# An attention and gated-MLP kernel: the last chunk's gate values kept in SBUF instead of DRAM, its last copies moved to ScalarE, its final adds split over GpSimd and VectorE

## The chip, the cores and the metric

The kernel runs on one core of a Trainium2 chip, in one launch. The metric is the device time of one execution in microseconds; the time before is the median of seven runs. The engines are named as in the profile: PE (TensorE), with its weight loads apart as PEld, DVE (VectorE), ACT (ScalarE), POOL (GpSimd) and SP (SyncE, which here only issues DMAs).

## The reference

All inputs and the output are bf16. With S = 2048 tokens, D = 640, 32 heads of 20 columns and F = 1728:

```python
xn = layernorm(x)
q, k, v = split(xn @ wqkv)                    # 32 heads of 20
o = softmax(q @ k.T * 20 ** -0.5) @ v         # every token with every token
s = o @ wo
h = sigmoid(xn @ w_gate) * (xn @ w_up)
g = silu(h @ w_down)
out = x + s * g
```

## The kernel before

**The tiling.** The tokens lie in four chunks of 512 (`QC`, index c), each of four token tiles of 128 (t4). The heads lie in eight groups of four (g). A *block* is one group with one chunk of queries: 32 blocks in all, in the order of the groups, but with the last two groups interleaved, so that the chunks end one after another; block 31 is the last group with the last chunk (c = 3). A block computes the scores of four heads against 16 key tiles on PE (L881, one matmul of 32 rows for each head, into the PSUM banks `scA` and `bk`), their exponentials, and the product with the values (L918, a *value group* of PE), which adds up in the PSUM bank `oacc`. v carries a column of ones, so row 0 of each head in `oacc` is the softmax's denominator.

**Two ways to the exponential.** Some of the score tiles go to ACT, which takes exp from PSUM (L120, output `pt`). The others go to DVE, which approximates exp on the bits of the numbers: one conversion to int16 for each 512 columns (L1214, output `iv`), and then three passes over up to four of them at a time (L966, L969, L972, output `pb`).

**What is put between.** The gated MLP runs as filler work on PE: for each chunk the gate and up products (L698, into `hT` over ACT's tanh and a product on DVE), then the down product (L736) for each token tile and each half of the 640 columns. `mk_down` ends with ACT's tanh of the result (L120, output `td`) and DVE's product (L746), which leaves the gate values times four, in fp32, in a small rotating tile `gqs`. A DMA on SP (L748) writes that tile to a DRAM scratch, `gq_dram`. For the chunks 0 to 2, `mk_out` later multiplies o with wo (L786), reads the gate values back (L772) and combines them with x (L793 on DVE, L796 on POOL), and L798 stores the result.

**The division.** After a block, DVE copies `oacc` to SBUF (L931). The denominators go through DRAM and a reciprocal (L941), come back broadcast (`rl`, L946), POOL multiplies (L948), and SP writes the result to `oU` (L956), which is the left operand of the product with wo. For block 31 this is done on the core instead, as the *chain*: DVE copies `oacc` (`e_on`, L1006), PE transposes (L1010), DVE takes the reciprocal (L760) and multiplies (L762), PE transposes back (L1019), and DVE copies the result to `o` (`e_o`, L1023).

**The end.** The output product of the last chunk lies in PSUM: 512 columns of each of the four token tiles in `mains` (two in `scA`, two in `bk`), and the remaining 128 columns of all four in one bank, `rest`. The `fill` list multiplies all heads but the last group's (L997), and `late_mm` adds the last group's (L1001), the rest first and then the mains. `tail_load` reads, for each of the four token tiles, x (L985) and the gate values (L986) from DRAM into the region of `wd`, which is free once the last down product is over. Then DVE multiplies the rest by the gates (L1043) and adds x (L1048), and for each token tile multiplies (L1052) and adds (L1055, tiles 0 to 2 on POOL, tile 3 on DVE). L1059 stores the four tiles, from SP and ACT in turn.

**What sets the order.** PE, ACT and DVE run in an order that a planner writes out when the program is built: it steps through time with a cost for each piece of work and takes, for each engine, what is ready. `PLAN` holds one row of its settings for each block; they take effect when the block becomes the first with scores still to claim. POOL and SP are not among the planner's engines: their instructions are placed by the scheduler, by what they depend on, and each of the two runs its own queue in order. Tiles from a pool rotate over a fixed number of buffers by their tag: `gqs` and `otmp` share one tag of three buffers, and the weight tiles of the projections share the tag `wp` of two, whose last users are the loads `load_wu` of the last two units and the matmuls on them (L558, and `qu`, whose results L607 writes to `qD`).

Of the kernel before, what the change touches and what calls it, by code (L numbers as in the profile page):

```python
# [10 lines left out]
FP32 = mybir.dt.float32  # L11
BF16 = mybir.dt.bfloat16
I16 = mybir.dt.int16
ACT = mybir.ActivationFunctionType
ALU = mybir.AluOpType
# [3 lines left out]
P = 128  # L19
HEADS = 32  # L20
GH = 4
NG = HEADS // GH
DH = 20
GC = GH * DH
QC = 512
# [47 lines left out]
)  # L73

LOG2E = 1.4426950408889634
# [14 lines left out]
def kernel(  # L90
# [11 lines left out]
    nc = tc.nc  # L102
    x2 = A_x[0] if len(A_x.shape) == 3 else A_x
    out2 = out[0] if len(out.shape) == 3 else out
    S, D = x2.shape
    assert D == HEADS * DH and S % QC == 0
    KD = D // P
# [4 lines left out]
    NQC = S // QC  # L112
    HD = D // 2
# [16 lines left out]
    wk = ctx.enter_context(tc.tile_pool(name="wk", bufs=2))  # L130

    gq_dram = dram.tile([S, D], FP32, name="gq_dram", tag="gqd", bufs=1)
# [8 lines left out]
    vts = [persist.tile([P, TT, 2 * GH, VW], BF16, name=f"v{i}") for i in range(2)]  # L141
# [97 lines left out]
    with tc.tile_pool(name="ln", bufs=2) as lp, \  # L239
# [159 lines left out]
        t = 0.0  # L399
# [19 lines left out]
    w2 = ctx.enter_context(tc.tile_pool(name="w2", bufs=2))  # L419
# [7 lines left out]
    oacc = psum.tile([P, QC], FP32, name="oacc", tag="oacc")  # L427
# [24 lines left out]

    out_tiles = {}
    xfl = xnT.rearrange("p c k q -> p (c k q)")

# [12 lines left out]
    NBLK = NG * NQC  # L468
# [11 lines left out]
    q_at = {0: 0.0}  # L480
# [247 lines left out]
    def mk_down(c, t4, h, at):  # L728
        st = {}
        tt = 4 * c + t4  # L730

        def alloc():
            st["ps"] = misc_ps()

        def mm(kf):
            nc.tensor.matmul(st["ps"][:, 0:HD], lhsT=hT[0:fsz[kf], kf, t4 * P:(t4 + 1) * P],  # L736
                             rhs=wd[0:fsz[kf], kf, h * HD:(h + 1) * HD],
                             start=(kf == 0), stop=(kf == NFT - 1))

        def th():  # L740
            st["td"] = w2.tile([P, HD], BF16, tag="td", bufs=2, name="td")
            act_imm(st["td"], st["ps"][:, 0:HD], ACT.Tanh, 0.25)

        def ev():
            gqs = w2.tile([P, HD], FP32, tag="gqs", bufs=3, name="gqs")
            nc.vector.scalar_tensor_tensor(out=gqs, in0=st["td"], scalar=1.0, in1=st["ps"][:, 0:HD],  # L746
                                           op0=ALU.add, op1=ALU.mult)
            nc.sync.dma_start(out=gq_dram[tt * P:(tt + 1) * P, h * HD:(h + 1) * HD], in_=gqs)  # L748
        return Item([("PE", alloc, [(0.14, lambda kf=kf: mm(kf)) for kf in range(NFT)]),
                     ("ACT", 0.32, th), ("DVE", 0.40, ev, "free", mark("d", c, t4, h))], at, pre=[("h", c, kf) for kf in range(NFT)])  # L750

# [62 lines left out]
    items = [mk_v(0, list(range(t, min(t + 3, TT))), 0.0) for t in range(4 * NVP, TT, 3)]  # L814
    for b in range(NBLK):
        g, c = gc(b)
# [21 lines left out]
    glu_items = [x for f in glu for x in f(0.0)]  # L838
# [7 lines left out]
    def base():  # L846
        while head_blk[0] < NBLK - 1 and not n_left[head_blk[0]]:
            head_blk[0] += 1
        return head_blk[0]
# [125 lines left out]
    wfl = wd.rearrange("p k s -> p (k s)")  # L975
    hfl = hT.rearrange("p k s -> p (k s)")
    EX = D - 512
    tail = []

    def tail_load():  # L980
        for t4 in range(4):
            r = slice(4 * (NQC - 1) * P + t4 * P, 4 * (NQC - 1) * P + (t4 + 1) * P)
            o2 = wfl[:, t4 * 3 * D:(t4 + 1) * 3 * D]
            tail.append((o2[:, 0:D], o2[:, D:3 * D].bitcast(FP32)))
            nc.sync.dma_start(out=tail[t4][0], in_=x2[r, :])  # L985
            nc.sync.dma_start(out=tail[t4][1], in_=gq_dram[r, :])  # L986

# [3 lines left out]
    mains = [scA[1][:, 0, :], scA[1][:, 1, :], bank[0], bank[1]]  # L991
    rest = bank[2]
    last = {}
# [9 lines left out]

    def e_on():
        last["on"] = w2.tile([P, QC], FP32, tag="on", bufs=2, name="on")
        nc.vector.tensor_copy(out=last["on"], in_=oacc)  # L1006

    def e_tr():
        for i in range(4):
# [10 lines left out]

    def e_o():
        last["o"] = w2.tile([GC, QC], BF16, tag="rl", bufs=1, name="o7")
        nc.vector.tensor_copy(out=last["o"], in_=last["t"][0:GC, 0:QC])  # L1023

    chain = [("DVE", 0.60, e_on), ("PE", 1.52, e_tr), ("DVE", 0.75, e_scale), ("PE", 0.42, e_back), ("DVE", 0.45, e_o)]
    fill = []
    for kds in (range(t_l - 1), range(t_l - 1, t_l + 1)):
        fill += [(t4 - 2, 0.2133, lambda t4=t4, kd=kd: early(mains[t4], t4, slice(0, 512), kd))
# [4 lines left out]
    def tail_steps():  # L1033
        for _, _, f in fill:
            f()
        for t4 in range(4):
            late_mm(rest[:, t4 * EX:(t4 + 1) * EX], t4, slice(512, D))
        for t4 in range(4):
            late_mm(mains[t4], t4, slice(0, 512))
        tmps = [hfl[:, t4 * 2 * D:t4 * 2 * D + 1024].bitcast(FP32) for t4 in range(4)]  # L1040
        xg = wfl[:, 0:12 * D].rearrange("p (t u) -> p t u", u=3 * D)
        tmp = hfl[:, 8 * D:8 * D + 8 * EX].bitcast(FP32)
        nc.vector.scalar_tensor_tensor(out=tmp.rearrange("p (t e) -> p t e", e=EX),  # L1043
                                       in0=rest.rearrange("p (t e) -> p t e", e=EX), scalar=0.25,
                                       in1=wfl[:, 0:12 * D].bitcast(FP32).rearrange(
                                           "p (t u) -> p t u", u=3 * D // 2)[:, :, D // 2 + 512:3 * D // 2],
                                       op0=ALU.mult, op1=ALU.mult)
        nc.vector.tensor_tensor(out=xg[:, :, 512:D], in0=tmp.rearrange("p (t e) -> p t e", e=EX),  # L1048
                                in1=xg[:, :, 512:D], op=ALU.add)
        for t4 in range(4):  # L1050
            xr, gqr = tail[t4]
            nc.vector.scalar_tensor_tensor(out=tmps[t4], in0=mains[t4], scalar=0.25, in1=gqr[:, 0:512],  # L1052
                                           op0=ALU.mult, op1=ALU.mult)
            add = nc.vector if t4 == 3 else nc.gpsimd
            add.tensor_tensor(out=xr[:, 0:512], in0=tmps[t4], in1=xr[:, 0:512], op=ALU.add)  # L1055
        for t4 in range(4):
            r = slice(4 * (NQC - 1) * P + t4 * P, 4 * (NQC - 1) * P + (t4 + 1) * P)
            eng = nc.sync if t4 % 2 == 0 else nc.scalar
            eng.dma_start(out=out2[r, :], in_=tail[t4][0])  # L1059

    with tc.manual_schedule(engines={ENG.PE, ENG.Activation, ENG.DVE}):
        nc.sync.dma_start(out=wo, in_=A_wo.rearrange("(kd p) e -> p kd e", p=P))
# [7 lines left out]
        now = 0.0  # L1070
# [13 lines left out]
        active = []  # L1084
# [38 lines left out]
        while chain or items or glu_items or any(it.i < len(it.ops) for it in active):  # L1123
# [3 lines left out]
            if bb > blk_loaded:  # L1127
                blk_loaded = bb
                rule.update(zip(KEYS, PLAN[bb]) if bb < len(PLAN) else ())
                g, c = gc(bb)  # L1130
                if c == 0 and g + 1 < PG:
                    spread_wst(g + 1, load_wst(g + 1))
                if c == 0 and g + 1 < NG:
                    if g % 2 == 1:
                        wvs[(g + 1) // 2] = load_wv((g + 1) // 2)
            if not tail and not glu_items and q_at.get(NBLK - 1, 1e9) <= now and not any(
                    it.need is None for it in items + active):
                tail_load()
            active = [it for it in active if it.i < len(it.ops)]
            if u_next < NU and base() >= (PG + u_next * UH // GH - 1) * NQC - 3 and (  # L1140
# [18 lines left out]
            for eng in ("ACT", "DVE"):  # L1159
# [15 lines left out]
                if it is not None:  # L1175
                    op = run_item(it, eng)
# [242 lines left out]
```

## Time and profile before

| what | value |
|---|---|
| median of 7 runs | 827.22 us (825.82 to 829.71) |
| profiled execution | 829.71 us, span 828.0 us |
| mean granted TensorE clock | 0.988 |
| instructions | 17089 |
| L120, `pt` from `scA` on ACT, x712 | 704.5 us busy |
| L1214, `iv` on DVE, x496 | 328.4 us busy |
| L881, score matmuls on PE, x1420 and x628 | 277.3 and 204.3 us busy |
| L1055, `wd` on POOL, x3 | 3.8 us busy |
| `gq_dram<-gqs` on SP | 32 issues, 160.0 KB each |
| DMA | 62.66 MB, mean 76 GB/s |

The profile is of one execution, and all positions in it are microseconds from the start of its span. "Busy" of PE counts matmuls that overlap in the pipeline. The chain of waits follows the work that ended last back from its end: each line has a start, a length, the engine, the tile written and the line. In the timeline, a bracket behind an instruction gives the idle time of its engine ahead of it and what released it. In the table of stretches, each column is an engine's busy time with the number of instructions in brackets, then the granted PE clock, the busy share of the DMA engines, and GB/s.

### The profile page before, as it was taken

The numbers are of one execution on the slowest core, as the hardware profiler recorded it, in microseconds if no ns is written. First come the engines' busy times: TensorE is split into PE (matmuls) and PEld (weight loads), VectorE is DVE, ScalarE is ACT, GpSimd is POOL, SyncE is SP. The second block draws the span as 40 slices with busy tenths as digits, with TensorE's granted clock in tenths as the row PEclk, the third lists the DMA queues.
The fourth block names the chain that finished last, engine by engine and source line by source line (L and its number), as shares of the span: only waits on it lengthen the run. The fifth ranks groups of instructions, "written<-read, shape, count | busy, mean of one in ns | idle before, by whom it ended". The sixth has DMA issues, their size and how long they took to land.

```text
span 828.0 us, 17089 instructions
## 1 busy us (share of the span) xinstructions
PE 787.2 (95%) x6420; PEld 269.6 (33%) x6420; DVE 780.6 (94%) x1230; ACT 785.5 (95%) x989; POOL 86.7 (10%) x90
## 2 busy tenths in 40 slices
PE   4799999999999999999999999999999999999994
PEld 2432222333333333333323222333333223333331
DVE  7689999999999999999999999999999999999992
ACT  7699999999999999999999999999999999999970
POOL 5000000000000000000000010000000002131141
PEclk9899999999999999999999999999999999999997
DMA  5611221123221232222112213331321124322214
GB/s 156 192 35 47 65 80 43 52 64 78 61 69 52 69 83 73 75 54 74 44 50 69 69 50 83 90 93 46 86 63 55 52 81 128 104 79 93 65 57 146
DMA packets 94899, 62.66 MB, mean 76 GB/s; under 512 B 36356, under 2 KB 88196, under 8 KB 94816
## 3 DMA queue, kind: packets, MB, share of 16 engines
q1 hardware_dynamic: 94528, 61.24, 26.4%
q8 instruction: 50, 0.82, 0.4%
q10 hardware_dynamic: 288, 0.33, 0.1%
q14 instruction: 33, 0.27, 0.1%
HBM read 46.59 MB, written 12.40 MB: 71 GB/s over the span
## 4 chain that ended last, share of the span: by engine, by line
PE 40%; ACT 30%; DVE 21%; issue 6%; DMA 2%; SPq 1%; POOL 0%; POOLq 0%; DVEq 0%; ACTq 0%
ACT pt L120 27%; PE scA L881 12%; PE oacc L918 8%; DVE iv L1214 8%; PE bk L698 8%; DVE pb L972 4%; PE bk L736 4%; DVE pb L966 2%; DVE pb L969 2%; PE bk L666 2%; PE bk L558 1%; ACT tnh L120 1%; PE bk L786 1%; DVE hT L706 1%; PE bk L881 1%
## 5 line engine op out<-in xcount | busy, mean ns | idle before, releaser
L120 ACT ACTIVATE pt<-scA 128x1024 bf16<-128x1024 f32 x712 | 704.5, 1149 | 7.7 <-PE bk L881 4.5
L1214 DVE TENSOR_SCALAR iv<-bk 128x512 int16<-128x512 f32 x496 | 328.4, 678 | 12.2 <-PE bk L881 11.3
L881 PE MATMUL scA<-q,kT 32*128 32x512 bf16 x1420 | 277.3, 384 | 7.8 <-ACT pt L120 3.7
L881 PE MATMUL bk<-q,kT 32*128 32x512 bf16 x628 | 204.3, 384 | 1.0 <-DVE iv L1214 0.7
L918 PE MATMUL oacc<-pt,v 128*21 128x512 bf16 x1552 | 182.0, 383 | 0.0
L881 PEld LDWEIGHTS <-kT 32*128 32x128 bf16 x2048 | 85.5, 91 | 261.8 <-issue 251.2
L918 PE MATMUL oacc<-pb,v 128*21 128x512 bf16 x992 | 156.5, 382 | 0.4 <-DVE pb L972 0.3
L972 DVE TENSOR_TENSOR pb<-iv,pb 128x2048 bf16<-128x2048 bf16 x124 | 154.4, 1246 | 0.7
L698 PE MATMUL bk<-xnT,wgu 128*128 128x512 bf16 x520 | 150.2, 383 | 2.1 <-DVE iv L1214 1.1
L948 POOL TENSOR_TENSOR on_bf<-on,rl 128x512 bf16<-128x512 f32 x31 | 46.2, 1489 | 665.3 <-DMA rl<-rd 396.9
L120 ACT ACTIVATE pt<-bk 128x512 bf16<-128x512 f32 x132 | 95.0, 720 | 1.4 <-PE bk L881 1.1
L966 DVE TENSOR_SCALAR pb<-iv 128x2048 int16<-128x2048 int16 x124 | 89.9, 725 | 1.2
L969 DVE TENSOR_SCALAR pb<-iv 128x2048 int16<-128x2048 int16 x124 | 90.9, 733 | 0.0
L736 PE MATMUL bk<-wd,hT 128*128 128x320 bf16 x448 | 88.1, 303 | 1.1 <-DVE iv L1214 0.9
L918 PEld LDWEIGHTS <-v 128*21 128x21 bf16 x2544 | 50.0, 91 | 88.9 <-issue 64.8
L698 PEld LDWEIGHTS <-wgu 128*128 128x128 bf16 x520 | 36.7, 97 | 66.5 <-issue 51.0
L736 PEld LDWEIGHTS <-hT 128*128 128x128 bf16 x448 | 34.1, 97 | 47.1 <-issue 38.9
L558 PE MATMUL bk<-xnT,wu 128*128 128x512 bf16 x160 | 47.0, 383 | 0.3 <-DVE iv L1214 0.3
L120 ACT ACTIVATE tnh<-bk 128x512 bf16<-128x512 f32 (+1 forms) x56 | 41.0, 731 | 0.1
L706 DVE SCALAR_TENSOR_TENSOR hT<-tnh,bk 128x512 bf16<-128x512 bf16 x52 | 35.2, 678 | 1.5 <-PE bk L698 0.8
L666 PE MATMUL bk<-wv,xnT 128*128 128x160 bf16 x280 | 29.5, 247 | 0.7 <-DVE iv L1214 0.6
L796 POOL TENSOR_TENSOR xnT<-otmp,xnT 128x320 bf16<-128x320 f32 x24 | 23.5, 987 | 46.9 <-DVE otmp L793 46.8
(105 smaller groups left out, 364.7 us busy)
## 6 DMA issues: line engine op xcount, KB each, us to landing
rl<-rd SPq DMA_DIRECT2D x124, 64.0 KB
wgu<-in_B_w_gate_dram SPq DMA_DIRECT2D x24, 320.0 KB
wgu<-in_B_w_up_dram SPq DMA_DIRECT2D x24, 320.0 KB
gq_dram<-gqs SPq DMA_DIRECT2D x32, 160.0 KB
xnT<-gq_dram SPq DMA_DIRECT2D x12, 320.0 KB
xt<-in_A_x_dram SPq DMA_DIRECT2D x16, 160.0 KB
oU<-on_bf SPq DMA_DIRECT2D x108, 20.0 KB
wd<-in_B_w_down_dram SPq DMA_DIRECT2D x1, 2080.0 KB
```

The source lines that it names most:

```text
L120: return nc.scalar.add_instruction(mybir.InstActivation(func=func, name=nc.get_next_instruction_name(), engine=ENG.Activation, ins=[nc.sca ...
L558: nc.tensor.matmul(st["ps"], lhsT=wus[u][:, kd, i, :], rhs=xnT[:, c, kd, :], start=(kd == 0), stop=(kd == KD - 1))
L666: nc.tensor.matmul(st["ps"][:, i * 2 * GC:(i + 1) * 2 * GC], lhsT=xn_tok(tts[i], kd), rhs=wvs[pr][:, kd, :], start=(kd == 0), stop=(kd == ...
L698: nc.tensor.matmul(st[key][0:fs, :], lhsT=w[:, i, kd, ko * P:ko * P + fs], rhs=xnT[:, c, kd, :], start=(kd == 0), stop=(kd == KD - 1))
L736: nc.tensor.matmul(st["ps"][:, 0:HD], lhsT=hT[0:fsz[kf], kf, t4 * P:(t4 + 1) * P], rhs=wd[0:fsz[kf], kf, h * HD:(h + 1) * HD], start=(kf = ...
L881: nc.tensor.matmul(dst, lhsT=kTs[gc(b)[0] % 2][32 * j:32 * j + 32, kt * P:(kt + 1) * P], rhs=qts[b % 3][32 * j:32 * j + 32, :], start=True ...
L918: nc.tensor.matmul(oacc[32 * j:32 * j + DH + 1, :], lhsT=lhsT, rhs=u["src"], start=first, stop=last, tile_position=(0, 32 * j), skip_group ...
L948: nc.gpsimd.tensor_tensor(out=on_bf, in0=on, in1=rl, op=ALU.mult)
L966: nc.vector.tensor_scalar(out=pb[:, 0, :, :].bitcast(I16), in0=iv, scalar1=0x7F80, scalar2=1, op0=ALU.bitwise_and, op1=ALU.bitwise_or)
L969: nc.vector.tensor_scalar(out=pb[:, 1, :, :].bitcast(I16), in0=iv, scalar1=0x007F, scalar2=0x3F00, op0=ALU.bitwise_and, op1=ALU.bitwise_or)
L972: nc.vector.tensor_tensor(out=pb[:, 1, :, :], in0=iv.bitcast(BF16), in1=pb[:, 1, :, :], op=ALU.mult)
L1214: nc.vector.tensor_scalar(out=d["iv"][:, j, :], in0=bank[bk], scalar1=B_OFF, scalar2=0.0, op0=ALU.add, op1=ALU.max)
```

## The change

There are five edits:

- `mk_down`: for the last chunk the result of L746 goes straight to SBUF that has no further use, token tiles 0 and 1 to the last quarter of `xnT`, tiles 2 and 3 to the first buffer of the values, `vts[0]`. The DMA to `gq_dram` is left out for this chunk.
- `tail_load`: reads x alone, two token tiles to a buffer of the tag `wp`, and is called from block 28 on, where before it waited until all gated-MLP items and early fillers were done.
- The chain's copies `e_on` and `e_o` move from DVE to ACT, and the planner's list says so.
- The end: the rest is multiplied in two halves on DVE, and its two adds go to POOL; of the main adds, tiles 0 and 1 stay on POOL, and 2 and 3 are on DVE. The stores go in the order 0, 2, 1, 3.
- The last row of `PLAN`, in force for block 31, has other settings.

The lines of the changed program that the text names: L1014 (`e_on`), L1031 (`e_o`), L1009 (`late_mm`), L1052 (rest), L1055 (rest adds), L1059 (mains), L1062 (main adds).

```diff
-    (0.25, 4, 0.15, 0, 0, 0.2, 0.4, 1, -2.0, 2, 2, 2, 0, 1, 4),
+    (0.45, 4, 0.15, 0, 0.2, 0.2, 0.2, 1, -2.0, 2, 2, 0, 0, 1, 4),
...
+    vfl = vts[0].rearrange("p t h c -> p (t h c)")
+    gq_last = [xfl[:, 3 * KD * QC:3 * KD * QC + 4 * D].bitcast(FP32), vfl[:, 0:4 * D].bitcast(FP32)]
...
-            gqs = w2.tile([P, HD], FP32, tag="gqs", bufs=3, name="gqs")
+            if c == NQC - 1:
+                gqs = gq_last[t4 // 2][:, t4 % 2 * D + h * HD:t4 % 2 * D + (h + 1) * HD]
+            else:
+                gqs = w2.tile([P, HD], FP32, tag="gqs", bufs=3, name="gqs")
...
-            nc.sync.dma_start(out=gq_dram[tt * P:(tt + 1) * P, h * HD:(h + 1) * HD], in_=gqs)
+            if c < NQC - 1:
+                nc.sync.dma_start(out=gq_dram[tt * P:(tt + 1) * P, h * HD:(h + 1) * HD], in_=gqs)
...
-            o2 = wfl[:, t4 * 3 * D:(t4 + 1) * 3 * D]
-            tail.append((o2[:, 0:D], o2[:, D:3 * D].bitcast(FP32)))
-            nc.sync.dma_start(out=tail[t4][0], in_=x2[r, :])
-            nc.sync.dma_start(out=tail[t4][1], in_=gq_dram[r, :])
+            if t4 % 2 == 0:
+                w = wk.tile([P, 2 * KD, GH, 32], BF16, tag="wp", bufs=2, name="xr")
+                xr_last.append(w.rearrange("p a j e -> p (a j e)").rearrange("p (t u) -> p t u", u=D))
+            tail.append(xr_last[t4 // 2][:, t4 % 2, :])
+            nc.sync.dma_start(out=tail[t4], in_=x2[r, :])
...
-        nc.vector.tensor_copy(out=last["on"], in_=oacc)
+        nc.scalar.copy(out=last["on"], in_=oacc)
...
-        nc.vector.tensor_copy(out=last["o"], in_=last["t"][0:GC, 0:QC])
+        nc.scalar.copy(out=last["o"], in_=last["t"][0:GC, 0:QC])
-    chain = [("DVE", 0.60, e_on), ("PE", 1.52, e_tr), ("DVE", 0.75, e_scale), ("PE", 0.42, e_back), ("DVE", 0.45, e_o)]
+    chain = [("ACT", 0.48, e_on), ("PE", 1.52, e_tr), ("DVE", 0.75, e_scale), ("PE", 0.42, e_back), ("ACT", 0.48, e_o)]
...
-        nc.vector.scalar_tensor_tensor(out=tmp.rearrange("p (t e) -> p t e", e=EX),
...
-        nc.vector.tensor_tensor(out=xg[:, :, 512:D], in0=tmp.rearrange("p (t e) -> p t e", e=EX),
-                                in1=xg[:, :, 512:D], op=ALU.add)
+        for i in range(2):
+            nc.vector.scalar_tensor_tensor(out=tmp[:, 2 * i:2 * i + 2, :], in0=rests[:, 2 * i:2 * i + 2, :], scalar=0.25,
+                                           in1=gq_last[i].rearrange("p (t u) -> p t u", u=D)[:, :, 512:D],
+                                           op0=ALU.mult, op1=ALU.mult)
+            nc.gpsimd.tensor_tensor(out=xr_last[i][:, :, 512:D], in0=tmp[:, 2 * i:2 * i + 2, :],
+                                    in1=xr_last[i][:, :, 512:D], op=ALU.add)
...
-            add = nc.vector if t4 == 3 else nc.gpsimd
+            add = nc.vector if t4 > 1 else nc.gpsimd
...
-        for t4 in range(4):
+        for i, t4 in enumerate((0, 2, 1, 3)):
...
-            eng = nc.sync if t4 % 2 == 0 else nc.scalar
-            eng.dma_start(out=out2[r, :], in_=tail[t4][0])
+            eng = nc.sync if i % 2 == 0 else nc.scalar
+            eng.dma_start(out=out2[r, :], in_=tail[t4])
...
-            if not tail and not glu_items and q_at.get(NBLK - 1, 1e9) <= now and not any(
-                    it.need is None for it in items + active):
+            if not tail and base() >= NBLK - 4:
                 tail_load()
```

More of the change, by code (lines that the diff above doesn't have):

```diff
@@ L977 @@
     EX = D - 512
-    tail = []
+    tail, xr_last = [], []
     def tail_load():
@@ L1040, in tail_steps @@
         tmps = [hfl[:, t4 * 2 * D:t4 * 2 * D + 1024].bitcast(FP32) for t4 in range(4)]
[L1041 to L1047, printed above, removed]
@@ L1048, in tail_steps @@
-        nc.vector.tensor_tensor(out=xg[:, :, 512:D], in0=tmp.rearrange("p (t e) -> p t e", e=EX),
-                                in1=xg[:, :, 512:D], op=ALU.add)
+        tmp = hfl[:, 8 * D:8 * D + 8 * EX].bitcast(FP32).rearrange("p (t e) -> p t e", e=EX)
+        rests = rest.rearrange("p (t e) -> p t e", e=EX)
+        for i in range(2):
[4 more added lines that the diff above has]
+                                    in1=xr_last[i][:, :, 512:D], op=ALU.add)
@@ L1050, in tail_steps @@
         for t4 in range(4):
-            xr, gqr = tail[t4]
-            nc.vector.scalar_tensor_tensor(out=tmps[t4], in0=mains[t4], scalar=0.25, in1=gqr[:, 0:512],
+            gqr = gq_last[t4 // 2][:, t4 % 2 * D:t4 % 2 * D + 512]
+            nc.vector.scalar_tensor_tensor(out=tmps[t4], in0=mains[t4], scalar=0.25, in1=gqr,
                                            op0=ALU.mult, op1=ALU.mult)
-            add = nc.vector if t4 == 3 else nc.gpsimd
-            add.tensor_tensor(out=xr[:, 0:512], in0=tmps[t4], in1=xr[:, 0:512], op=ALU.add)
@@ L1056, in tail_steps @@
-        for t4 in range(4):
+            add = nc.vector if t4 > 1 else nc.gpsimd
+            add.tensor_tensor(out=tail[t4][:, 0:512], in0=tmps[t4], in1=tail[t4][:, 0:512], op=ALU.add)
+        for i, t4 in enumerate((0, 2, 1, 3)):
             r = slice(4 * (NQC - 1) * P + t4 * P, 4 * (NQC - 1) * P + (t4 + 1) * P)
-            eng = nc.sync if t4 % 2 == 0 else nc.scalar
-            eng.dma_start(out=out2[r, :], in_=tail[t4][0])
+            eng = nc.sync if i % 2 == 0 else nc.scalar
+            eng.dma_start(out=out2[r, :], in_=tail[t4])
```

## The prediction

> **What bounds the kernel now.** First the page's busy line of each engine, to see whether one engine rules:
>
> ```profile
> PE 787.2 (95%) x6420; PEld 269.6 (33%) x6420; DVE 780.6 (94%) x1230; ACT 785.5 (95%) x989; POOL 86.7 (10%) x90
> ```
>
> None does: PE, DVE and ACT are all full, so time can only come from a stretch where all three stand still. The table of busy time by stretches (sum, one row per window) finds it:
>
> ```profile
> 790.00:800.00 10.00, 9.89 (x90) 3.53 (x88) 10.00 (x17) 9.94 (x13) 5.31 (x5) 1.00 0.14 47
> 804.20:815.70 11.50, 11.41 (x73) 5.75 (x72) 2.66 (x6) 0.56 (x2) 1.08 (x1) 1.00 0.49 157
> 815.70:828.00 12.30, 0.01 (x1) 0.00 (x0) 4.93 (x7) 0.00 (x0) 3.82 (x3) 0.64 0.30 100
> ```
>
> Up to 804.2 all three work; to 815.7 PE alone sets the pace; then 12.3 us pass without PE. The chain of waits, at its end, says who owns those:
>
> ```profile
> 811.96 2.57 PE bk L997 x12
> 815.70 3.14 DMA wd<-gq_dram
> 820.63 1.30 DVE hT L1052 x2
> 822.52 1.15 POOL wd L1055
> 823.67 1.56 POOLq L1414
> ```
>
> and the timeline of that stretch (start, length, engine, line) gives the terms:
>
> ```profile
> 814.46 0.40 PE L1001 MATMUL bk<-wo_l,o 80*128 80x128 bf16 x4
> 815.70 0.32 SPq L986 DMA_DIRECT2D wd<-gq_dram  x1
> 819.11 0.69 DVE L1043 SCALAR_TENSOR_TENSOR hT<-bk,wd 128x512 f32<-128x512 f32 x1 [10.71 <-DMA wd<-gq_dram]
> 819.84 0.69 DVE L1048 TENSOR_TENSOR wd<-hT,wd 128x512 bf16<-128x512 f32 x1
> 821.40 3.82 POOL L1055 TENSOR_TENSOR wd<-hT,wd 128x512 bf16<-128x512 f32 x3 [16.12 <-DVE hT L1052]
> 823.15 1.07 DVE L1055 TENSOR_TENSOR wd<-hT,wd 128x512 bf16<-128x512 f32 x1
> ```
>
> The reader should see that VectorE starts its last work at 819.11, though the matmuls that it needs (the four of L1001 from 814.46, the fourth at 814.63) were over before 815. What came last is the read-back of the gate values: the last gate half is written at 811.95, it has landed at 815.62, the read is issued at 815.70 and lands at 818.83.
>
> **Term 1: the trip through DRAM.** The change keeps these values in SBUF. The order of the changed program's instructions shows the first rest operation (L1052) waiting on PE alone. L760, another VectorE reader of PSUM, starts 0.31 us after the start of the last 128-column matmul ahead of it (805.95 to 806.26), so the rest can start at 814.63 + 0.31 = 814.94 instead of 819.11: **-4.17 us**. This stall goes whole, for the x rows that are still loaded now come hundreds of us earlier. What is late next is VectorE and GpSimd themselves.
>
> **Term 2: the adds.** Before, from 819.11 to the last output issue at 825.25: 6.14 us, closed by GpSimd's third add (three in 3.82 us). After, the order on VectorE is: two rest halves (256 columns each), two mains, main 2 and its add, main 3 and its add; GpSimd has two rest adds and the adds of chunks 0 and 1. VectorE repeats a 512-column L1052 every 0.60 us; 256 columns less is about 0.27 off that (0.48 for the 320 columns of L793 against 0.69 for 512 gives the slope), so 0.33. That puts the mains at 815.60, 816.20 and 816.80, done at 817.48. An add on VectorE took 0.69 with GpSimd idle (L1048) and 1.07 beside it (L1055). GpSimd: 320-column adds (L796) took 0.79 undisturbed, 0.99 in the mean; I take 0.77 for 256, so its rest adds run 815.43 to 816.95. Its 512-column adds took 1.15 beside L1052 and 1.60 beside VectorE's add. Chunk 0 then ends at 818.1 to 818.55, chunk 1 at 819.65 to 820.1; VectorE's add 2 ends at 818.2 to 818.6, main 3 at 818.9 to 819.3, add 3 at 820.05 to 820.43. The middle, 820.27, is 5.33 us after 814.94: **-0.81 us**. Bounds: all adds undisturbed, 820.0 (-1.1); GpSimd's four adds each at its slow price (1.17, 1.17, 1.60, 1.60 from 815.43), 820.97 (-0.1). Behind that nothing changes: the last store lands 1.79 us after its issue and the program ends 0.95 later, as before.
>
> A rule speaks against this part. The Trainium skill (SBUF — State Buffer, "SBUF: two separate sides") holds that VectorE with two SBUF inputs and GpSimd lock each other out for a whole instruction. By that the four main adds go one after the other, 1.15 + 0.69 + 1.15 + 0.69 from 816.95, and the last ends at 820.6 rather than 820.27, so the sum would be 0.36 us poorer. The trace has half of each: VectorE's 1.07 is 0.38 over 0.69, and started 0.52 before GpSimd's second add was over.
>
> **Term 3: the last block's order.** The planner's new row and the moved copies change the instruction orders from 784.75 on, nowhere earlier on PE, ACT and VectorE. Counted from there to the first L997 (807.36): PE has 15 score groups, 6 value groups, 15 others, where it had 16, 7, 15, with the same matmuls. A change of kind costs 0.11 (eight L918 last 0.545 to the next start, two rounds of 0.216 and the rest), and that is 0.2 to 0.5 us less PE time. VectorE loses one iv (0.60), and its last three passes run on 1536 columns instead of 2048, a quarter off 0.60 + 0.60 + 1.15: 1.2 us less. ACT gains one 512-column exp piece, 0.45 (0.905 for two, in steady state). Before, ACT's last exp ended at 802.41 and VectorE's last pass at 804.14, and the last value group went at 804.20. Now they end at about 802.9 and 802.95, and the last group goes at about 803.2: -1.0.
>
> From that group to the first L997 it took 3.16 us. Now the copy of oacc runs on ACT, 0.43 after the group starts, for 0.62 (ACT's 128x512 reads of PSUM took 0.60 to 0.69), so the transposes start after 1.2 us instead of 1.43. But td of the last-but-one gate half is queued on ACT behind that copy, and its VectorE product (L746, 0.49) stands ahead of the reciprocal on VectorE: td ends at 1.40, the product runs from 1.5, the reciprocal starts at about 1.9 where its transposes are ready at 1.8, then 0.84 to the back transposes and 0.66 for these and three L736: 3.4 to 3.55. So +0.3, and **-0.65 us** in all. Lower bound -1.4, the idle steps that I add up on PE before 807.36; upper +0.4, as L969 ran 1.03 and 1.28 instead of 0.68 where GpSimd worked beside it, and two such hits can fall on the last passes. From L997 to 815.72 PE has the same 48 matmuls in the same order: nothing. The ACT copy of o has 6 us of room. oU's DMAs of block 30 landed at 810.26, just before use; in the new order rl's four issues are no longer behind an output store that waits for GpSimd (796.64 to 799.22), so they come earlier.
>
> **What costs nothing.** The eight dropped gate writes were issued on SP, off the chain. The four x loads now stand in SP's queue in two pairs, each behind lt and ahead of the fourth qD write, waiting for PE's last reader of the wp buffer. Those matmuls were over by 457.1 and 552.3, the qD writes next in line went at 458.31 and 553.32, and a pair takes about 0.75 us to issue. Both fit. The covers if not: the next wgu load (472.49) is first used at 484.1, 11.6 us of room.
>
> **Sum.** -4.17 - 0.81 - 0.65 = -5.63 us. Profiled execution: span 828.0, time 829.71, so 824.1 there; that run was the slowest of seven. From the median 827.22: **821.6 us**.
>
> **Rivals.**
> 1. The forecast, with its bounds: best -4.17 - 1.1 - 1.4 = -6.7 (820.5), worst -4.17 - 0.1 + 0.4 = -3.9 (823.3). Chance 0.80 with the run-to-run spread.
> 2. The new order of block 31 is worse than I count: one more wait of an exp piece on each of its last turns, 1 to 2 us beyond the upper bound of term 3, gives 824.3 to 825.4. For: the three engines are within 0.5 us of each other, so a slip on any shows. Against: each has less work or room. 0.08.
> 3. A wait takes the place of the one removed: ACT's copy of oacc must wait for eight DMA semaphores, where VectorE's waited for PE alone. If one belongs to block 30's oU writes, the copy starts at 810.3 instead of 804.8, and PE's queue waits in order at the transposes: 5.5 us in place of term 3, -4.17 - 0.81 + 5.5 = +0.5, so 827.7, no change. Against: the tiles that it reuses were freed a block earlier. 0.05.
> 4. Slower: the x loads hold SP. The source asks for them at block 28, some 250 us after their place in the queue. If the head of SP's queue waits like that, wgu loads behind it come late; 11.6 us are covered, and beyond 11.6 + 5.6 + 1.65 = 19 us of hold the kernel is slower by over 0.2% (1.65 us, about what a measurement of this kernel can tell from no change). A hold of 25 us gives 835. Against: the wait is on PE's early matmuls, seen above. 0.03.
>
> The remaining 0.04 is better than 819.8. The range 819.8 to 824.2 takes the bounds of rival 1, 820.5 to 823.3, and 0.7 to 0.9 us for the spread of medians (the seven runs span 825.82 to 829.71). Faster 0.92, same 0.05, slower 0.03.
>
> **What would show it.** Right: L1052 starts 0.3 us after the fourth rest matmul with no DMA wait; from there 5.1 to 6.0 us to the last output issue; the last L1009 matmul 0.3 to 1.2 us earlier than 815.7; SP's x loads issued near 457 and 552. Wrong: a gap on PE ahead of the transposes of over 0.5 us (rival 3), a VectorE or GpSimd add over 1.6, or a late wgu load after 457.

## The result and the profile after

The changed kernel takes 823.72 us (median of 14 runs, 822.07 to 825.61); the kernel before, timed beside it, takes 826.72 us (35 runs, 824.68 to 829.71). The ratio is 0.9962, with a 95% interval of 0.9951 to 0.9972: faster by 3.1 us (2.3 to 4.1), or 0.4%, where 5.6 were forecast.

The profiled execution after took 821.95 us, with a span of 820.2 us at a mean granted clock of 0.995; before it was 829.71, 828.0 and 0.988. These 7.8 us are not the effect. The two executions are 3.67 us apart after their first 46 us, where nothing was changed: 1.46 of it stood at 34 us already, and 2.21 came while the PE clock stood at half, for 10.24 us before and for 3.41 us after. So I compare stretches that lie behind that point. The busy line of each engine shows that little was taken from any engine:

```profile
PE 783.3 (95%) x6419; PEld 267.1 (33%) x6419; DVE 780.0 (95%) x1228; ACT 786.8 (96%) x991; POOL 84.5 (10%) x91
```

The stretches are cut at events that both programs have. The first, S1, goes from the first output product of chunk 2 on PE (L786, after L792) to the first product of `fill` (L997, after L1005). The second, S2, goes from there to the start of the last product of `late_mm` (L1001, after L1009). The third, S3, goes on to the end. The table of busy time by stretches, of the kernel before, has these rows (window and length, then PE, PEld, DVE, ACT, POOL, the granted PE clock, the DMA share, GB/s):

```profile
781.35:807.36 26.01, 25.70 (x231) 10.21 (x231) 24.60 (x40) 21.75 (x28) 10.95 (x9) 1.00 0.19 64
807.36:815.34 7.98, 7.98 (x51) 3.83 (x49) 0.82 (x2) 0.12 (x1) 0.00 (x0) 1.00 0.65 208
815.34:828.00 12.66, 0.38 (x2) 0.00 (x0) 4.93 (x7) 0.00 (x0) 3.82 (x3) 0.65 0.32 108
```

and of the changed kernel:

```profile
777.75:804.70 26.95, 26.19 (x230) 10.13 (x229) 24.43 (x38) 22.89 (x29) 10.66 (x9) 1.00 0.19 58
804.70:812.69 7.99, 7.99 (x49) 3.84 (x48) 0.94 (x3) 0.55 (x2) 0.00 (x0) 1.00 0.00 0
812.69:820.20 7.51, 0.38 (x2) 0.00 (x0) 4.50 (x7) 0.00 (x0) 3.96 (x4) 0.69 0.24 87
```

Three things are to be seen. S3 lost 5.1 us. S2 did not move. S1 grew by 0.94 us, although DVE has two instructions and 0.17 us less to do in it: the forecast had it shrink by 0.65. From a fixed exponential ahead of S1 to the end, the profiles of the kernel before measure 85.40 and 86.21 us, those of the changed one 81.89 and 81.56, which is -4.1 us.

The end of the timeline after shows what took the place of the read-back:

```profile
811.80 0.40 PE L1009 MATMUL bk<-wo_l,o 80*128 80x128 bf16 x4
812.24 0.42 DVE L1052 SCALAR_TENSOR_TENSOR hT<-bk,xnT 128x256 f32<-128x256 f32 x1 [6.47 <-PE bk L1009]
812.74 1.29 POOL L1055 TENSOR_TENSOR xr<-hT,xr 128x256 bf16<-128x256 f32 x2 [13.51 <-DVE hT L1052]
814.00 2.71 POOL L1062 TENSOR_TENSOR xr<-hT,xr 128x512 bf16<-128x512 f32 x2
814.82 0.88 DVE L1062 TENSOR_TENSOR xr<-hT,xr 128x512 bf16<-128x512 f32 x1
815.77 1.85 ACTq L1066 DMA_DIRECT2D out_dram<-xr  x2
816.33 0.93 DVE L1062 TENSOR_TENSOR xr<-hT,xr 128x512 bf16<-128x512 f32 x1
```

VectorE's rest now waits for PE alone: it starts at 812.24, 0.26 us after the start of the fourth small matmul (811.98 in the trace). The last store is issued at 817.29, 5.05 us later. The chain of waits, at its end, says the same, and where the path ran before it (start, length, engine, tile, line):

```profile
797.98 1.67 DVE pb L972
...
804.76 1.40 PE scA L1005 x6
...
812.24 0.75 DVE hT L1052 x2
812.99 1.80 DVE hT L1059 x3
814.82 0.88 DVE xr L1062
815.70 0.61 DVE hT L1059
816.33 0.93 DVE xr L1062
```

There is no DMA in this end of it any more. What is new stands at the top: one bit pass (L966 before, L972 after) on 1536 columns took 1.67 us and lies on the path.

### The profile page after: what moved, and what is told of

It is laid out like the page before. It is cut to its first block, busy times and chain, and to the rows that moved or that the text cites. A ratio compares the mean times of both kernels' runs of the same rounds, so it can differ in the third digit from the quotient of the medians.

```text
span 820.2 us, 17053 instructions
## 1 busy us (share of the span) xinstructions
PE 783.3 (95%) x6419; PEld 267.1 (33%) x6419; DVE 780.0 (95%) x1228; ACT 786.8 (96%) x991; POOL 84.5 (10%) x91
## 5 line engine op out<-in xcount | busy, mean ns | idle before, releaser
L978 DVE TENSOR_TENSOR pb<-iv,pb 128x2048 bf16<-128x2048 bf16 x124 | 155.0, 1250 | 0.7
L954 POOL TENSOR_TENSOR on_bf<-on,rl 128x512 bf16<-128x512 f32 x31 | 43.3, 1396 | 660.1 <-DMA rl<-rd 331.3
L972 DVE TENSOR_SCALAR pb<-iv 128x2048 int16<-128x2048 int16 x124 | 92.0, 742 | 1.2
L738 PE MATMUL bk<-wd,hT 128*128 128x320 bf16 x448 | 88.4, 302 | 0.9 <-DVE iv L1220 0.7
L975 DVE TENSOR_SCALAR pb<-iv 128x2048 int16<-128x2048 int16 x124 | 89.1, 719 | 0.0
L738 PEld LDWEIGHTS <-hT 128*128 128x128 bf16 x448 | 34.2, 97 | 45.8 <-issue 37.6
```

Of the source, the lines that this page charges most:

```text
L954: nc.gpsimd.tensor_tensor(out=on_bf, in0=on, in1=rl, op=ALU.mult)
L972: nc.vector.tensor_scalar(out=pb[:, 0, :, :].bitcast(I16), in0=iv, scalar1=0x7F80, scalar2=1, op0=ALU.bitwise_and, op1=ALU.bitwise_or)
L975: nc.vector.tensor_scalar(out=pb[:, 1, :, :].bitcast(I16), in0=iv, scalar1=0x007F, scalar2=0x3F00, op0=ALU.bitwise_and, op1=ALU.bitwise_or)
L978: nc.vector.tensor_tensor(out=pb[:, 1, :, :], in0=iv.bitcast(BF16), in1=pb[:, 1, :, :], op=ALU.mult)
```

## The experiments

The question was where 1.6 us (S1 +0.94 instead of -0.65) went. In the timelines of S1, the bit passes of DVE that end long are those that run beside an instruction of GpSimd. Before (DVE by itself, then POOL; L796 is the add of the output of chunk 2, L948 the multiply of a block's division):

```profile
792.07 1.03 DVE L969 TENSOR_SCALAR pb<-iv 128x2048 int16<-128x2048 int16 x1
798.07 1.28 DVE L969 TENSOR_SCALAR pb<-iv 128x2048 int16<-128x2048 int16 x1
802.92 1.23 DVE L972 TENSOR_TENSOR pb<-iv,pb 128x2048 bf16<-128x2048 bf16 x1
...
803.03 2.25 POOL L948 TENSOR_TENSOR on_bf<-on,rl 128x512 bf16<-128x512 f32 x1 [4.23 <-DMA rl<-rd]
```

After (L972, L975 and L978 are the passes now, L954 the multiply):

```profile
781.36 1.25 DVE L975 TENSOR_SCALAR pb<-iv 128x2048 int16<-128x2048 int16 x1
787.45 1.28 DVE L972 TENSOR_SCALAR pb<-iv 128x2048 int16<-128x2048 int16 x1
794.91 0.90 DVE L975 TENSOR_SCALAR pb<-iv 128x2048 int16<-128x2048 int16 x1
797.98 1.67 DVE L972 TENSOR_SCALAR pb<-iv 128x1536 int16<-128x1536 int16 x1
...
797.96 1.28 POOL L954 TENSOR_TENSOR on_bf<-on,rl 128x512 bf16<-128x512 f32 x1
```

Alone, a pass takes 0.68 (the first two) or 1.21 us (the third) on 2048 columns, and 0.55 or 0.96 on 1536. I call the sum of what the passes of S1 take beyond that the *loss*: before 0.35 + 0.22 + 0.60 + 0.02 = 1.2 (the rows above, and a third pass of 1.43), after 0.57 + 0.60 + 0.20 + 0.22 + 1.12 = 2.7 (the rows above, and a third pass of 1.41).

The theory was that this loss is the missing 1.6 us. The rivals were that the copies on ACT or the planner's new row cost it, that the eight dropped writes on SP let other transfers come earlier, and that it is mere scatter between executions. All runs are in one table; "timed" is the ratio to the kernel before with its interval, or the times themselves where there was one.

| run | S1 | loss | S1 less loss | S2 + S3 | span, clock | timed |
|---|---|---|---|---|---|---|
| before | 26.01 | 1.17 | 24.84 | 20.63 | 828.0, 0.988 | – |
| e7_before_again * | 26.01 | 1.17 | 24.84 | 20.68 | 824.7, 0.992 | 0.9994 (0.9973 to 1.0015) |
| after | 26.94 | 2.70 | 24.24 | 15.55 | 820.2, 0.995 | 0.9962 (0.9951 to 0.9972) |
| e0_changed_again * | 26.95 | 2.71 | 24.24 | 15.55 | 821.9, 0.998 | 0.9937 (0.9916 to 0.9958) |
| e1_gates_only * | 27.99 | 3.18 | 24.81 | 16.60 | 823.4, 0.997 | 0.9982 (0.9965 to 0.9999) |
| e6_writes_kept * | 27.99 | 3.17 | 24.82 | 16.57 | 824.3, 0.995 | 0.9985 (0.9966 to 1.0004) |
| e3_old_row * | 28.08 | 3.18 | 24.90 | 15.56 | 825.4, 0.990 | 0.9965 (0.9941 to 0.9988) |
| e4_copies_dve * | 26.87 | 2.71 | 24.16 | 15.72 | 819.7, 0.995 | 821.36 us, one run |
| e5_mul30_dve * | 26.38 | 1.61 | 24.77 | 16.38 | 822.4, 0.994 | 0.9954 (0.9935 to 0.9973) |
| e8_bf16_products * | 26.38 | 1.59 | 24.79 | 16.11 | 819.9, 0.996 | 0.9926 (0.9900 to 0.9951) |
| e9_nudge | 26.63 | 2.37 | 24.26 | 15.84 | 819.3, 0.995 | 0.9946 (0.9925 to 0.9968) |
| e10_bf16_nudge | 26.04 | 1.26 | 24.78 | 15.19 | 818.0, 0.998 | 0.9940 (0.9918 to 0.9962) |

In the eight runs marked * the trace lacks the record of the first `fill` product, at which S1 ends. The changed kernel has ten records of these products into `scA` in its first profile and nine in its second (`after`, then `e0_changed_again`):

```profile
L1005 PE MATMUL scA<-wo,oU x10: 379/379/390, 804.7 to 808.9; 128*128 128x512 bf16 x8, 48*128 48x512 bf16 x2
L1005 PE MATMUL scA<-wo,oU x9: 379/379/389, 806.6 to 810.6; 128*128 128x512 bf16 x7, 48*128 48x512 bf16 x2
```

Where the record is there, the second product starts 0.22 us behind the first. So in these eight rows S1 is 0.22 shorter, and S2 + S3 0.22 longer, than the first recorded product gives. The expectations below quote some of them as recorded (28.21 for e1, 26.6 for e5).

S2 and S3 are added up here, because in e4, e7 and e9 the PE clock was already halved at about 811 (813 to 819 in the others), ahead of the last late matmuls: that makes S2 0.7 to 0.9 us longer (7.98 in all others), most of which S3 gives back.

**The kernels again.** The first is the changed kernel once more, with no edit:

> The changed kernel once more, unchanged. In its first profile the stretch from the first output product of chunk 2 (L792) to the first of the last chunk (L1005) was 26.94 us (before: 26.01), and from the start of the last late matmul to the end 7.56 (before: 12.65). If the lengthening of the first stretch comes from VectorE's passes that meet GpSimd's adds by accident, it should scatter by some tenths from one execution to the next; if it comes from the order of the instructions, it should be 26.94 within 0.1. The end should be 7.56 within 0.1 either way. Time against the kernel before: 0.9945 to 0.997.

Measured: S1 26.95, loss 2.71, ratio 0.9937. The passes lost the same, and the same ones were hit, so the encounters belong to the program and not to the execution. The second is the kernel before once more:

> The kernel before, once more, for a second profile of it and for the spread of its time against itself. Theory of the port: the first stretch (first output product of chunk 2 to the first of the last chunk) is 24.9 us, as far as the order of the instructions goes, plus what VectorE's passes lose beside GpSimd, which was 1.17 us in the first profile: 26.0 again within 0.3, and the end 12.65 within 0.2. If the 26.01 was an accident of one execution, the stretch is elsewhere, up to the 28.2 of the kernel with the gates alone. Ratio 1.000 within 0.002.

Measured: ratio 0.9994, loss 1.17 again, S1 26.01. A second profile of either program thus moves S1 by 0.01 at most, so the growth of 0.94 is no scatter between executions.

**The gates alone.** The values stay in SBUF, with the x rows loaded early and the rest in two halves, and all else is as before: the old row, copies, engines of the final adds and order of the stores.

```diff
-    (0.45, 4, 0.15, 0, 0.2, 0.2, 0.2, 1, -2.0, 2, 2, 0, 0, 1, 4),
+    (0.25, 4, 0.15, 0, 0, 0.2, 0.4, 1, -2.0, 2, 2, 2, 0, 1, 4),
...
-        nc.scalar.copy(out=last["on"], in_=oacc)
+        nc.vector.tensor_copy(out=last["on"], in_=oacc)
...
-            nc.gpsimd.tensor_tensor(out=xr_last[i][:, :, 512:D], ...
+            nc.vector.tensor_tensor(out=xr_last[i][:, :, 512:D], ...
-            add = nc.vector if t4 > 1 else nc.gpsimd
+            add = nc.vector if t4 == 3 else nc.gpsimd
...
```

> The gates of the last chunk in SBUF and the early x loads alone: the old planner row, the copies on VectorE, the rest adds and main 3's add on VectorE and mains 0 to 2 on GpSimd as before. If the trip through DRAM is worth what the profile of before says, the end goes from 12.65 to 12.65 - 4.17 = 8.5 us, and the first stretch stays at 26.0. If the new row, copies and adds give nothing, the time is that of the changed kernel within 0.1%; if they give the 0.8 us of the adds and cost 0.9 in the first stretch, it is the same too, but with 8.5 and 26.0 instead of 7.56 and 26.9. Ratio to before 0.994 to 0.997.

Measured: S3 8.62 after 12.65 before, -4.03, the size of term 1. But the ratio is 0.9982, hardly faster, because S1 grew by 1.98 us with the *old* planner row, as much as the loss did (3.18 for 1.17). So neither the new row nor the copies brought the encounters; the edit that keeps the gates in SBUF did. The dearest one, in the timeline of this kernel:

```profile
801.23 1.29 POOL L954 TENSOR_TENSOR on_bf<-on,rl 128x512 bf16<-128x512 f32 x1 [3.92 <-DMA rl<-rd]
...
801.43 2.17 DVE L978 TENSOR_TENSOR pb<-iv,pb 128x2048 bf16<-128x2048 bf16 x1
```

It is the same pair as before at 802.92 and 803.03, with the parts exchanged. Before, DVE began 0.11 ahead; its last pass took 1.23, and GpSimd's multiply stretched to 2.25 at no cost to anyone. Here GpSimd began 0.20 ahead, took its 1.29, and the pass took 2.17, at the place where the last value group waits for it.

**The multiply of block 30 on DVE.** In the changed kernel it is held back and done by DVE ahead of the last block's copy.

```diff
+        if b == NBLK - 2:
+            pend.append((g, c, on, rl))
+            return
+        norm_c(nc.gpsimd, g, c, on, rl)
...
     def e_on():
+        norm_c(nc.vector, *pend.pop())
```

> The changed kernel, with block 30's multiplication by the reciprocals moved from GpSimd to VectorE, behind VectorE's last pass. Theory of the port: in the changed kernel this GpSimd instruction (1.28 us from 797.96) held up VectorE's pass L972, 1.67 us instead of 0.55; without it the last pass ends 1.1 us earlier, the first stretch is 25.8 to 26.1 instead of 26.94, and the time is 0.9 to 1.1 us (0.12%) shorter. Theory of the order: the first stretch is long because the planner's new row and the copy on ACT make PE wait; then it stays at 26.9, or grows by up to the 0.7 us that the multiplication takes on VectorE.

The timeline of DVE in this kernel:

```profile
799.87 0.56 DVE L980 TENSOR_SCALAR pb<-iv 128x1536 int16<-128x1536 int16 x1
...
800.93 0.96 DVE L986 TENSOR_TENSOR pb<-iv,pb 128x1536 bf16<-128x1536 bf16 x1
801.80 0.68 DVE L962 TENSOR_TENSOR on_bf<-on,rl 128x512 bf16<-128x512 f32 x1
```

The last passes are undisturbed, and the pass that took 1.67 takes 0.56. The loss fell by 1.1 us to 1.61, but S1 by 0.56 only. The last pass now ends 22.25 us after the start of S1 (23.36 in the changed kernel), and ACT's last exponential ends at 22.44 in both: the end moved from DVE to ACT. The price of an encounter on the path is thus what is next behind it, not its whole length. The last store took 2.65 us to land in this profile, where 1.8 is usual, and that is the 0.8 us in S2 + S3. The timed ratio, 0.9954, does not stand out from the changed kernel's.

**The old row.** The changed kernel with the old last row of `PLAN`, and nothing else.

```diff
-    (0.45, 4, 0.15, 0, 0.2, 0.2, 0.2, 1, -2.0, 2, 2, 0, 0, 1, 4),
+    (0.25, 4, 0.15, 0, 0, 0.2, 0.4, 1, -2.0, 2, 2, 2, 0, 1, 4),
```

> The changed kernel with the planner's old row for block 31; the copies stay on ACT. Theory of the order: the first stretch falls back to 26.0 or below. Theory of the port: it goes with the sum of what the passes lose beside GpSimd (1.2 us before, 2.7 in the changed kernel): about 24.8 plus that sum, whichever row is used. The end stays at 7.56.

Measured: S1 28.08, loss 3.18. Against the two runs of the changed kernel the new row is worth 1.1 us of S1: 0.5 in the loss, and the remainder in the order itself. Against e1 it isolates the engines of the final adds and the order of the stores (with the copies on ACT, priced below): S2 + S3 is 15.56 for 16.60, -1.04.

**The writes kept.** The gates alone as in e1, but SP writes the last chunk's values to `gq_dram` as before, though nobody reads them.

```diff
-            if c < NQC - 1:
-                nc.sync.dma_start(out=gq_dram[tt * P:(tt + 1) * P, h * HD:(h + 1) * HD], in_=gqs)
+            nc.sync.dma_start(out=gq_dram[tt * P:(tt + 1) * P, h * HD:(h + 1) * HD], in_=gqs)
```

> The kernel with the gates alone (old row, copies on VectorE, old adds), but the last chunk's gate values are also written to the DRAM scratch as before, from their new place; nobody reads them. Without these writes its first stretch was 28.21 us, 3.18 of it lost by the passes, against 26.01 and 1.17 before. Theory of the port, with SP's queue as the cause of the new encounters: with the writes back, SP issues everything at its old places, and the first stretch returns to 26.0 to 26.5. Rival: the encounters come from the buffers, since otmp now has all three of its tag to itself, or from a few hundredths of a us in the start of each GpSimd add; then the stretch stays above 27.5. The end stays at 8.6 in both.

Measured: S1 27.99 and loss 3.17, as in e1 to the hundredth. The dropped writes have no part in it. What remains of the gate edit is the early x loads, issued over 200 us ahead of S1, and the new place of the values, which no longer use the rotating tag that they shared with `otmp`, the output's products. No run parts these two; that it is the tag is argued from the trace. In the trace before, the first add of chunk 2 waits for two semaphores, DVE's and POOL's own, and begins 0.145 us after its product; without the values in the rotation it waits for DVE's alone and begins 0.08 after. The second add is queued behind it, and its start decides who is first at the next pass. In the kernel before (e7), POOL and then DVE:

```profile
780.86 2.11 POOL L796 TENSOR_TENSOR xnT<-otmp,xnT 128x320 bf16<-128x320 f32 x2 [10.15 <-DVE otmp L793]
...
781.63 0.68 DVE L969 TENSOR_SCALAR pb<-iv 128x2048 int16<-128x2048 int16 x1
```

The second of the two adds begins at 781.609 in the trace, 0.020 us ahead of the pass, and yet the pass takes its 0.68 and the add 1.35. In e6 the add begins at 783.279, 0.090 ahead of the pass, and takes 0.79, and the pass takes 1.25. I take it that all that follows in S1 is shifted by this; the nudge below tests only that a shift of this size is enough.

**The copies.** The changed kernel with `e_on` and `e_o` back on DVE.

```diff
-        nc.scalar.copy(out=last["on"], in_=oacc)
+        nc.vector.tensor_copy(out=last["on"], in_=oacc)
...
```

> The changed kernel with the two copies of the last division back on VectorE (new row, new adds). The prediction costed the copy on ACT at about +0.3 us between the last value group and the first output product of the last chunk, which took 3.15 us before and 3.53 in the changed kernel: here 3.15 to 3.3. Theory of the port: the passes meet GpSimd where they did in the changed kernel (2.7 us), so the first stretch is 26.9 to 27.2 less 0.3. End 7.56.

Measured: from the last value group to the first `fill` product 3.46 us, where the changed kernel has 3.53 and the kernel before 3.16. I had expected it to fall back to 3.15 to 3.3; it did not, so the copies on ACT cost 0.07. The rest goes with the new row: in every run with it, 15 down products (L736 before, L738 after) stand in that way, 0.14 us apart, and 13 in every run with the old one. In e3, with the old row and the copies on ACT, the way took 3.25. S1, 26.87, is that of the changed kernel less the 0.07.

**Narrower products.** e5 with the products of tiles 2 and 3, which DVE adds itself, in bf16 instead of fp32. This rounds them once more than the kernel before.

```diff
-        tmps = [hfl[:, t4 * 2 * D:t4 * 2 * D + 1024].bitcast(FP32) for t4 in range(4)]
+        tmps = [hfl[:, t4 * 2 * D:t4 * 2 * D + 1024].bitcast(FP32) if t4 < 2
+                else hfl[:, t4 * 2 * D:t4 * 2 * D + 512] for t4 in range(4)]
```

> The kernel with block 30's multiplication on VectorE, and besides the products of the last two token tiles stored in bf16 instead of fp32, so that VectorE's two main adds have bf16 operands alone. If the two adds (0.88 and 0.92 us) drop to about 0.5, the last store is issued 0.6 to 0.8 us earlier unless GpSimd's second main add (ends 0.6 us ahead of VectorE's last add) or the store behind it is then last: the end goes from 7.57 to 7.0 or 7.2. The first stretch stays at 26.6. Time 0.5 us under that of the kernel with the multiplication alone.

Measured: DVE's two main adds take 0.61 and 0.66 us instead of 0.88 and 0.93, and the last store is issued 4.52 us after the rest's start instead of 5.05. It landed in 2.9 us in this profile, so S2 + S3 (16.11) does not show the gain. The timed ratio, 0.9926 (0.9900 to 0.9951), is the lowest of all, but its six runs also had the highest mean clock (0.996, where the changed kernel's had 0.993), so the time does not show the gain either.

**A nudge.** If hundredths of a microsecond decide the first encounter, a delay on GpSimd should turn it. The changed kernel, with a one-column copy on GpSimd ahead of each add of chunk 2:

```diff
+            if tt // 4 == 2 and add is nc.gpsimd:
+                nc.gpsimd.tensor_copy(out=nudge[:, tt % 4 * 2 + h:tt % 4 * 2 + h + 1], in_=tmp[:, 0:1])
             add.tensor_tensor(out=xr[:, sl], in0=tmp, in1=xr[:, sl], op=ALU.add)
```

> The changed kernel; ahead of each of GpSimd's eight adds of chunk 2 stands a copy of one column of the same product, so that the add itself starts some 0.1 to 0.2 us later; nothing else is moved on any engine. Theory of the port (who comes first has it): the first two adds came 0.08 us behind their product, and the second 0.09 us ahead of VectorE's pass L975, which then took 1.26 us; in the kernel before the lead was 0.02 and that pass took 0.68. With the nudge the pass is first and takes 0.68, other encounters change sides too, and the sum that the passes lose moves from 2.7 by at least 0.5 us, most likely downward; the first stretch is 24.35 us plus that sum within 0.3. Theory of the order alone: a tenth of a us on GpSimd, which is idle most of the time, changes nothing, 27.0 to 27.2.

The timeline of DVE in this kernel:

```profile
780.43 0.68 DVE L978 TENSOR_SCALAR pb<-iv 128x2048 int16<-128x2048 int16 x1
...
797.23 1.64 DVE L978 TENSOR_SCALAR pb<-iv 128x1536 int16<-128x1536 int16 x1
```

The first encounter is turned: 0.68 for 1.25, by *adding* work on GpSimd. The whole loss fell by 0.33 us only, where I had expected 0.5 or more, since block 30's multiply met another pass instead (1.64 for 0.55). S1 is 26.63, 0.31 less.

**Both together.** e8 with the nudge.

> The kernel with block 30's multiplication on VectorE and the bf16 products, with the same nudge of GpSimd's adds. There ACT's last exp and not VectorE's last pass ended last, and the passes still lost 1.6 us beside the adds. If the nudge takes at least 0.5 of that away and ACT's gaps of 0.6 and 0.4 us come from it, the first stretch falls from 26.6 to 25.6 to 26.2; if ACT's gaps are the order's, it stays at 26.5 to 26.6. The end 7.2 to 7.6 when the last store lands in 1.8 us as in most runs. Ratio to before 0.992 to 0.995.

Measured: loss 1.26, S1 26.04, S2 + S3 15.19. Against e8 the nudge takes 0.33 from the loss and 0.34 from S1. It is the shortest kernel by stretches: from the fixed exponential to the end 80.53 us, against 81.56 and 81.89 of the changed kernel and 85.40 and 86.21 of the kernel before. By time it is 0.9940 (0.9918 to 0.9962), which is below the kernel before and cannot be told from the changed kernel (0.9937 and 0.9962).

## Why the prediction was right and wrong

**The time.** The sign is right, and 823.72 lies in the stated range of 819.8 to 824.2, but there luck had a part: the worst sum of the terms was -3.9 (823.3), -3.1 was measured, and only the allowance for the spread of medians covers the rest. The forecast of -5.6 is 1.8 times the effect. By the stretches the sum is -5.1 + 0.9 = -4.2: two terms held, and the third failed.

**Term 1, the trip through DRAM: right.** -4.17 forecast, -4.03 measured alone (e1). The rest starts 0.26 us after the fourth small matmul, with no DMA wait, where 0.31 was forecast. That is -4.22 for the wait itself; in e1 0.19 comes back behind it, in the rest's halves and behind the last issue.

**Term 2, the adds: right, somewhat too small.** -0.81 forecast with -1.1 to -0.1 around it; -1.04 measured (e3 beside e1). The last store was issued 5.05 us after L1052's start, just under the 5.1 to 6.0 that I gave and at the bound with all adds undisturbed: DVE's adds took 0.88 and 0.93, less than the 1.07 beside GpSimd that I had counted with, and POOL's 256-column adds 0.67 instead of 0.77. By the exclusive lock of the Trainium skill (SBUF — State Buffer, "SBUF: two separate sides") this part was to be 0.36 poorer than my sum. The part came out 0.23 better than my sum. The rule's price was not paid in full: from 814.00, one after the other, 1.15 + 0.69 + 1.15 would put the end of GpSimd's second add at 816.99, and the trace has it at 816.71.

**Terms 1 and 2 together:** -4.98 forecast, -5.1 measured in S3: -4.22 for the wait, -1.09 from the rest's start to the last issue (5.05 for 6.14), and +0.22 behind it, where I had no change (2.96 us to the end for 2.74).

**Term 3, the last block's order: wrong, in size and sign.** -0.65 forecast, +0.9 measured in S1. The count of the order itself holds up: what S1 takes less its loss is 24.81 to 24.90 in the five runs with the old row, and 24.16 to 24.26 in the four with the new one that end on DVE's last pass, a difference of 0.62 between the means. (This is a subtraction. e5 showed that not all of a loss comes back when it is removed, as ACT's last exponential then ends last.) That exponential also ended 0.9 us later in S1 than I had counted, 22.44 for 21.55. With the nudge it ended at 21.86 (e9) and 21.84 (e10), so 0.6 of the 0.9 goes with the encounters too; the remainder was not isolated.

The step that failed is the upper bound of the term. I had seen L969 run 1.03 and 1.28 beside GpSimd, and treated more of the like as a mishap worth at most two hits. The loss went from 1.2 to 2.7 us, through five hits instead of three, one of them 1.12 on a pass of 0.55. That S1 is longer by what the passes lose is shown by e1 and e6 (with the old order, loss +2.0 and S1 +1.98) and by the nudge (loss -0.33, S1 -0.31 and -0.34), and that the multiply of block 30 makes its hit by e5. The sentence that `rl` comes earlier, given there as harmless, was half of the mechanism: with `rl` already landed (797.57), the multiply starts at 797.96 right behind an add, in the middle of the last passes, where before it came at 803.03, 0.11 behind the start of the last one.

**The eight dropped writes cost nothing:** shown by e6. **The copies on ACT:** 3.4 to 3.55 us from the last value group to the first `fill` product forecast, 3.53 measured. The number came out by luck: the copies cost 0.07 of it (e4), and two more down products under the new row the rest.

**The rivals.** No DMA semaphore held ACT's copy: it began at 801.64, 0.47 after the last value group. The four x loads did not hold SP: they were issued from 453.5 to 549.3 with 0.36 to 0.42 us each. The rival in which the order of the last block turns out worse came halfway: S1's +0.94 lies 0.5 beyond the upper bound, where it had 1 to 2, and it came through GpSimd's encounters, not through an order that is worse by itself.

**What stays open.** The stretches give -4.1 us, the timed medians -3.1 with an interval whose end is at -4.1. Between executions the time varies by several microseconds with the mean granted clock (about 0.5 us for each 0.001, fitted over all runs); at equal clock the changed kernel is 3.0 ± 0.5 us ahead (95%). The remaining microsecond has no place in any stretch that I looked at. By the same fit e1 is 0.9 ± 0.6 and e6 0.6 ± 0.7 us ahead, where the same stretch gives 1.8 for both (83.94 and 84.01 us), so it seems to be missing without the new row, copies and adds too. Single profiles cannot place it ahead of that stretch: two executions of the changed kernel reach the same exponential 2.0 us apart (738.36 and 740.36).

## What to carry to other kernels

When a stretch is bound by VectorE's passes, list GpSimd's instructions that run in it, and price each by what it does to the pass that it meets, not by its own length: which of the two starts first is worth more than a microsecond and can turn on 0.1 us. An edit that only changes where a value is kept or when a transfer lands moves those meetings, so a sum of such small terms needs a range that holds several hits to either side. A stall that ends a program, with nothing beside it, could here be priced to a tenth of a microsecond from one timeline. Before two profiles are compared at an event, count its records in both: one missing matmul looked like 0.22 us of scatter.

## What the runs showed of the hardware

**Whoever starts first, nearly.** The Trainium skill (SBUF — State Buffer, "SBUF: two separate sides") says that of a VectorE instruction in a 2-port fast mode, or with two SBUF inputs, and a GpSimd instruction that reads SBUF, the one that starts first holds the shared port pair for its whole length, while the other blocks. Of the runs here, e1 (GpSimd 0.20 ahead: 1.29 and the pass 2.17 for 1.21) and the kernel before (DVE 0.11 ahead: 1.23, and GpSimd 2.25 for 1.28) agree. By the starts that the trace records it is not exact: the add that was 0.020 ahead (e7) lost, the one 0.090 ahead (e6) won. In one later encounter an add began 0.16 behind the start of a third pass, in e7 and e6 alike. The pass took its 1.21 in both, but the add took 2.31 in e7, where the next pass took 0.68, and 1.70 in e6, where the next pass took 1.28; what decided there stays open.

**The clock at the start.** The PE clock stood at half for 10.24 us from 33.97 in one execution (before) and for 3.41 us from 33.85 in another (after), with the same instructions up to there, and 2.21 us came between the two meanwhile. Of the twelve profiles two show 10.24 us, two 3.41 us, and eight no such stretch.

**The last store.** The 160 KB of a token tile's store usually land 1.8 us after their issue; in two of the twelve profiles the last one took 2.65 and 2.9.
